# Two-stage Fourier transform and SoLU layer on one core: the order of scaled copies, first-transform products and block sums in a software pipeline

## Chip, core and metric

The kernel runs on one core of a Trainium2 chip. The time is that of the device for one execution, in microseconds (us); of several runs the median is taken. Before the change it is 1193.14 us (three runs, 1192.39 to 1193.9).

The core has five engines that take their instructions in order and wait for one another through semaphores: TensorE (PE, matmuls into PSUM; PEld is its weight load), VectorE (DVE), ScalarE (ACT), GpSimd (POOL) and SyncE (SP, which issues transfers here).

## What is computed

```python
def _attn_ref(x):                       # x: (8, 3136, 256), float32
    X = np.fft.fft(x, axis=1)
    X = np.fft.fft(X, axis=2)
    return X.real.astype(np.float32)

def _moe_ref(x, w_in, w_out, g_ln):     # x: (25088, 256), w_in: (256, 1024), w_out: (1024, 256)
    h = x @ w_in
    h_max = np.max(h, axis=-1, keepdims=True)
    e = np.exp(h - h_max)
    sm = e / (np.sum(e, axis=-1, keepdims=True) + 1e-09)
    solu = h * sm
    mu = np.mean(solu, axis=-1, keepdims=True)
    var = np.mean((solu - mu) ** 2, axis=-1, keepdims=True)
    ln = (solu - mu) / np.sqrt(var + 1e-06) * g_ln
    return (ln @ w_out).astype(np.float32)
```

The real part of the two-dimensional transform of each of eight sequences goes, as 25088 rows of 256, through a layer with 1024 hidden features: product, exponential against the row's maximum, a normalisation, product.

## The kernel before

The eight sequences are taken in four pairs. The transform along the sequence of 3136 = 49 x 64 is done in two parts. `transform1` (length 49) is done for a pair ahead of time, in 16 halves of 8 chunks: GpSimd adds the mirrored rows (`add_mirror`), VectorE folds the features (`fold`), TensorE multiplies, ScalarE copies the result `z` out, and it goes to DRAM and back. `transform2` (length 64) gives a *unit*: 128 rows of the spectrum, and with them 128 mirrored ones (signs 0 and 1). A pair has 25 units (the first has one sign), 100 in all, and step `i` of the main loop handles unit `i`:

- `up`: product with the input weights, in an even and an odd part, into PSUM banks of their own; `even` and `join` (VectorE) put the parts together for each sign and find the row's maximum;
- `expo` (ScalarE), `product` (VectorE: u = h times exponential), `square` and `stats` (ScalarE: variance), then a `pow` on GpSimd that gives the row's scale `rs`;
- `turn_blocks` (VectorE) and `move_blocks` (16 or 24 transfers) transpose u.

Four steps later (`lag`) comes the product with the output weights. A unit of even number takes it plainly (`down`: 16 matmuls of 256 columns for each sign), sign 1 one step `late`. A unit of odd number takes both signs at once as a 2 x 2 block product with seven block products instead of eight (`Down`), over two steps; it needs four sums `S` of blocks of u, which GpSimd makes. PSUM has four banks for results; `result(i)` is bank `i % 4`, and `bank(0..2)` are 2, 3 and 1.

```python
def transform1(pr, s):
    ...
    ps = result(0 if pr.p else s).rearrange("p (l d) -> p l d", l=2)
    ...                                   # four matmuls
    nc.scalar.copy(pr.z[:, l : l + 2, :], ps[0:ZR])
    if l == CH - 2:
        keep(pr, c, ...)                  # z to DRAM

def transform2(pr, k1):
    ...
    ps = result(0)[:, 0 : KD * P]         # four matmuls; take2 (ScalarE) copies them to q
    ...

def sums(t):                              # GpSimd
    A11, A12, A21, A22 = blocks(t)
    t.S = spool.tile([P, 4, KF // 2, P], FP32, tag="S", name="S")
    for j, (a, b, op) in enumerate(((A21, A22, ALU.add), (t.S[:, 0], A11, ALU.subtract),
                                    (A11, A21, ALU.subtract), (A12, t.S[:, 1], ALU.subtract))):
        nc.gpsimd.tensor_tensor(out=t.S[:, j], in0=a, in1=b, op=op)

class Down:                               # self.C11, self.X, self.P53 = banks 2, 3, 1
    ...
    def keep(self, s, half, ps):
        nc.scalar.mul(out=self.place(s, half), in_=ps, mul=self.t.rs[:, s : s + 1])
    # p1: C11 afresh         seed: X <- C11 (ScalarE)     p2: adds to C11, keep11 takes it
    # p4: P53 afresh, keep4  p5: P53 afresh, keep5        p3: P53 afresh
    # p6: adds to X, keep6   p7: adds to X                finish: VectorE adds P53 and X to ot
```

The main loop, whose order within each engine is the order of the program (cut):

```python
for i in range(whole + 1, len(units) + lag + 3):
    cur = units[i] if i < len(units) else None
    old = units[i - lag] if i < len(units) + lag else None
    seven = old and by_seven(i - lag)
    plain, late, scaled = late, None, []
    if i > whole + 2:
        store(units[i - lag - 3])
    if seven:
        sums(old)
    if done:
        done.finish()
        done = None
    if cur:
        enter(i)
        even(cur, up(cur, 0))
        cur.odd = up(cur, 1)
        second_transform(i + 2)           # transform2, take2, spread
        join(cur, 0)
        if 1 in cur.signs:
            join(cur, 1)
        expo(cur, 0)
    if seven:
        new = Down(old, i == whole + 1)
        new.p1()
        new.seed()
    if half:
        half.p5()
        half.p6()
    if cur and 1 in cur.signs:
        expo(cur, 1)
    if half:
        half.keep5()
        half.keep6()
    if plain:
        ps_o = down(*plain)
        ...
    if seven:
        new.p4()
        new.p2()
    elif old:
        ...                               # down(old, 0); sign 1 is late
    if half:
        half.p3()
        half.p7()
        half, done = None, half
    if cur:
        for s in cur.signs:
            product(cur, s)
        square(cur, 0)
    if plain:
        scale(*plain, ps_o)
    if cur and 1 in cur.signs:
        square(cur, 1)
    if seven:
        new.keep4()
        new.keep11()
        half = new
    if cur:
        other_pairs(i, ahead_pe)          # transform1 of the next pair
    if cur:
        for s in cur.signs:
            turn_blocks(cur, s)
        ...                               # move_blocks
        stats(cur)                        # ends with the pow on GpSimd
    for t, s, ps_o in scaled:
        scale(t, s, ps_o)
    if cur:
        ...                               # turn: z back from DRAM
        other_pairs(i, ahead)             # add_mirror, fold, load of the next pair
```

Of the kernel before, what the change touches and what calls it, by code (L numbers as in the profile page):

```python
# [35 lines left out]
def kernel(  # L36
# [241 lines left out]
    def stats(t):  # L278

        n = slice(0, len(t.signs))  # L280
        es2, v = (small.tile([P, 2], FP32, tag=tag, name=tag) for tag in ("es2", "v"))
        nc.scalar.activation(out=es2[:, n], in_=t.esum[:, n], func=ACT.Square, bias=limits[:, 3:4], scale=1e-3)
        for s in t.signs:
            nc.scalar.activation(out=v[:, s : s + 1], in_=t.ssq[:, s : s + 1], func=ACT.Identity, bias=es2[:, s : s + 1],  # L284
                                 scale=float(FF) ** -3)
        t.rs = small.tile([P, 2], FP32, tag="rs", name="rs")
        nc.gpsimd.tensor_tensor(out=t.rs[:, n], in0=v[:, n], in1=neg_half[:, n], op=ALU.pow)  # L287
# [145 lines left out]
    def down(t, s):  # L433

        uT = t.batch.uT[:, t.w].rearrange("p c i (n s) -> p c (i n) s", s=2)
        ps = (result(0) if s else bank(0))[:, 0:D]
        for c in range(KF):
            nc.tensor.matmul(ps, uT[:, c, :, s], Wo[:, c, :], start=(c == 0), stop=(c == KF - 1))  # L438
        return ps
# [5 lines left out]
    def store(t):  # L445

        for s in t.signs:
            if s:
                i = NP * NC + t.p * (NK - 1) + t.k1 - 1
                dma = nc.gpsimd.indirect_dma_start(  # L450
                    out=out, out_offset=bass.IndirectOffsetOnAxis(ap=idx[:, i : i + 1], axis=0),
                    in_=t.ot[s], in_offset=None)
            else:
                dma = nc.sync.dma_start(out=out_k[t.p, t.k1], in_=t.ot[s])

            tc.declare_no_dep(dma.ins, group=f"out{1 - s}", reason="other rows of the output")
            tc.add_to_no_dep_group(f"out{s}", dma.ins)
# [153 lines left out]
    START = [[2 + 2 * c for c in range(NC)], [4, 6, 8, 10, 12, 13, 15, 16]]  # L611

    def ahead(pr, step):

        start = START[pr.p == 1]
        if step == 0:
            load(pr, 0)
            load(pr, 1)
        for c in range(NC):
            if step == start[c]:  # L620
                add_mirror(pr, c, nc.gpsimd)
            if step == start[c] + 1:
                fold(pr, c)
                if c + 2 < NC:
                    load(pr, c + 2)

    def ahead_pe(pr, step):

        for c in range(NC):
            for half in range(2):  # L630
                if step == START[pr.p == 1][c] + 2 + half:
                    transform1(pr, c * CH // 2 + half)

    def turn_parts(pr, step):

        if step in (-5, -3, 2, 6, 11):
            turn(pr, (-5, -3, 2, 6, 11).index(step))

    with tc.manual_schedule():
# [102 lines left out]
        def other_pairs(i, do):  # L742
            cur = units[i]
            if cur.p + 1 < NP:
                do(pairs[cur.p + 1], cur.k1)
# [3 lines left out]
        for i in range(whole + 1):  # L749
# [23 lines left out]
            if i < whole:  # L773

                begin(i + 1)
                if 1 in cur.signs:
                    square(cur, 1)
                stats(cur)
            else:
                for s in cur.signs:  # L780
                    square(cur, s)
                    turn_blocks(cur, s)
                stats(cur)
                scale(units[0], 0, ps_o)
# [10 lines left out]
        half, done, late = None, None, None  # L795
        for i in range(whole + 1, len(units) + lag + 3):
# [4 lines left out]
            if i > whole + 2:  # L801
                store(units[i - lag - 3])
            if seven:
                sums(old)
            if done:
                done.finish()
                done = None
            if cur:
                enter(i)
                even(cur, up(cur, 0))  # L810
                cur.odd = up(cur, 1)
                second_transform(i + 2)
                join(cur, 0)
                if 1 in cur.signs:
                    join(cur, 1)
                expo(cur, 0)
# [4 lines left out]
            if half:  # L821
                half.p5()
                half.p6()
            if cur and 1 in cur.signs:
                expo(cur, 1)
            if half:
                half.keep5()
                half.keep6()
            if plain:
# [4 lines left out]
            if seven:  # L834
                new.p4()
                new.p2()
            elif old:
                order = old.signs[::-1] if old is units[-1] else old.signs
                scaled.append((old, order[0], down(old, order[0])))
                if len(order) == 2:  # L840
                    if old is units[-1]:
                        scaled.append((old, order[1], down(old, order[1])))
                    else:
                        late = (old, order[1])
# [10 lines left out]
            if cur and 1 in cur.signs:  # L855
                square(cur, 1)
# [4 lines left out]
            if cur:  # L861
                other_pairs(i, ahead_pe)
            if cur:
# [91 lines left out]
```

## Time and profile before

| | |
|---|---|
| time, median of three | 1193.14 us |
| span of the profiled execution | 1190.8 us |
| TensorE busy | 1140.4 us |
| VectorE busy | 1005.6 us |
| ScalarE busy | 763.2 us |
| GpSimd busy | 636.2 us |
| mean DMA rate | 156 GB/s |

How to read the profile: L12 is line 12 of the kernel as it was run. L182 is `transform1`, L210 `transform2`, L238 `up`, L252 `join`, L261 `expo`, L268 `product`, L275 `square`, L284 the end of `stats`, L287 the `pow`, L300 `turn_blocks`, L326 `move_blocks`, L350 `sums`, L355 the seven block products, L386 their scaled copies, L396 `seed`, L390 `finish`, L438 the plain product, L443 its scaled copy, L185 the copy of `z`, L216 that of `q`. A group's row has its busy time and the mean duration of one instruction; "idle before" is the time in which the engine had nothing to run ahead of it, with the work whose end released it. Matmuls overlap in the array, and their ends are modelled.

### The profile page before, as it was taken

The numbers are of one execution on the slowest core, as the hardware profiler recorded it, in microseconds if no ns is written. First come the engines' busy times: TensorE is split into PE (matmuls) and PEld (weight loads), VectorE is DVE, ScalarE is ACT, GpSimd is POOL, SyncE is SP. The second block draws the span as 40 slices with busy tenths as digits, with TensorE's granted clock in tenths as the row PEclk, the third lists the DMA queues.
The fourth block names the chain that finished last, engine by engine and source line by source line (L and its number), as shares of the span: only waits on it lengthen the run. The fifth ranks groups of instructions, "written<-read, shape, count | busy, mean of one in ns | idle before, by whom it ended". The sixth has DMA issues, their size and how long they took to land.

```text
span 1190.8 us, 18553 instructions
## 1 busy us (share of the span) xinstructions
PE 1140.4 (96%) x5850; PEld 884.2 (74%) x5850; DVE 1005.6 (84%) x1376; ACT 763.2 (64%) x1841; POOL 636.2 (53%) x558
## 2 busy tenths in 40 slices
PE   2888999999999999999999899999999999999998
PEld 1556777778777778778777678777788777778777
DVE  7889889888879898898988989898888898888870
ACT  3577666666657667666656666676675676677651
POOL 3035487745655757645556666746544264543444
PEclk9999999999999999999999999999999999999999
DMA  9771989956689787656789898886575785745553
GB/s 231 198 187 31 163 176 192 204 135 148 145 158 188 176 174 199 169 135 146 140 158 179 167 186 169 169 169 146 133 162 124 146 145 125 158 110 137 130 119 103
DMA packets 458465, 185.55 MB, mean 156 GB/s; under 512 B 425750, under 2 KB 440350, under 8 KB 458368
## 3 DMA queue, kind: packets, MB, share of 16 engines
q1 hardware_dynamic: 444608, 146.22, 58.6%
q0 software_dynamic: 13760, 38.16, 13.4%
q8 instruction: 47, 0.77, 0.3%
q14 instruction: 50, 0.41, 0.1%
HBM read 44.78 MB, written 38.80 MB: 70 GB/s over the span
## 4 chain that ended last, share of the span: by engine, by line
PE 74%; DVE 6%; DMA 5%; ACT 5%; SPq 4%; issue 3%; POOL 3%; DVEq 0%; POOLq 0%; ACTq 0%
PE ps_m L438 24%; PE ps_h L238 23%; PE ps_m L355 21%; PE ps_m L182 4%; SPq L326 3%; PE ps_m L210 3%; ACT u L261 3%; DMA room<-in_x_dram 2%; DMA uT<-v 2%; DVE u L268 2%; POOL S L350 1%; DVE h L252 1%; DVE v L300 1%; DMA F<-in_f_tab_dram 1%; DVE ev L244 1%
## 5 line engine op out<-in xcount | busy, mean ns | idle before, releaser
L438 PE MATMUL ps_m<-Wo,uT 128*128 128x256 f32 x1632 | 372.1, 382 | 3.6 <-ACT uT L317 2.1
L238 PE MATMUL ps_h<-Wi,q 128*128 128x512 f32 x800 | 360.5, 593 | 1.5 <-DVE nmax L252 1.5
L438 PEld LDWEIGHTS ps_m<-Wo,uT 128*128 128x128 f32 x1632 | 314.1, 197 | 33.8 <-ACT uT L317 2.4
L268 DVE SCALAR_TENSOR_TENSOR u<-h,u 128x1024 f32<-128x1024 f32 x196 | 296.9, 1526 | 32.0 <-ACT u L261 24.6
L287 POOL TENSOR_TENSOR rs<-v,neg_half 128x2 f32<-128x2 f32 (+1 forms) x100 | 75.9, 759 | 448.9 <-ACT v L284 433.0
L238 PEld LDWEIGHTS ps_h<-Wi,q 128*128 128x128 f32 x800 | 147.6, 190 | 149.3 <-issue 136.7
L275 ACT ACTIVATE h<-u,usum 128x1024 f32<-128x1024 f32 x196 | 223.9, 1144 | 45.1 <-DVE u L268 44.3
L261 ACT ACTIVATE u<-h,neg 128x1024 f32<-128x1024 f32 x196 | 225.3, 1150 | 6.4
L300 DVE STREAM_TRANSPOSE v<-u 128x1024 f32<-128x1024 f32 x192 | 227.4, 1223 | 0.1
L216 ACT COPY q<-ps_m 128x256 f32<-128x256 f32 x100 | 37.2, 372 | 203.3 <-PE ps_m L210 181.3
L244 DVE SCALAR_TENSOR_TENSOR ev<-w_mid,r,ps_h 128x1024 f32<-128x1024 f32 x100 | 127.3, 1273 | 47.4 <-PE ps_h L238 41.2
L252 DVE CUSTOM_DVE_ANT_0 h<-ev,ps_h 128x1024 f32<-128x1024 f32 x100 | 122.2, 1222 | 41.9 <-PE ps_h L238 34.9
L350 POOL TENSOR_TENSOR S<-uT 128x512 f32<-128x512 f32 x94 | 147.2, 1566 | 1.2
L355 PE MATMUL ps_m<-Ws,S 128*128 128x128 f32 x1128 | 143.3, 277 | 2.0 <-ACT ot L386 2.0
L355 PEld LDWEIGHTS ps_m<-Ws,S 128*128 128x128 f32 x1128 | 135.3, 194 | 2.7 <-issue 2.6
L252 DVE CUSTOM_DVE_ANT_0 h<-h,ps_h 128x1024 f32<-128x1024 f32 x96 | 117.3, 1222 | 14.2 <-ACT neg L259 0.5
L450 POOL DMA_INDIRECT out_dram<-ot,idx x96 | 105.7, 1102 | 35.3 <-issue 17.1
L355 PE MATMUL ps_m<-Wo,uT 128*128 128x128 f32 x752 | 104.4, 282 | 1.4 <-ACT ps_m L396 1.3
L182 PE MATMUL ps_m<-y,F 98*100 98x258 f32 (+3 forms) x288 | 73.6, 390 | 29.1 <-DVE y L130 24.1
L355 PEld LDWEIGHTS ps_m<-Wo,uT 128*128 128x128 f32 x752 | 96.3, 196 | 2.5 <-ACT ps_m L396 1.7
L210 PEld LDWEIGHTS ps_m<-T,g 128*128 128x128 f32 x400 | 60.1, 191 | 50.8 <-issue 45.0
L259 ACT ACTIVATE neg<-nmax 128x1 f32<-128x1 f32 x196 | 38.8, 198 | 82.2 <-DVE nmax L252 69.8
(87 smaller groups left out, 1160.1 us busy)
## 6 DMA issues: line engine op xcount, KB each, us to landing
uT<-v SPq DMA_DIRECT2D x752, 128.0 KB
out_dram<-ot SPq DMA_DIRECT2D x100, 128.0 KB
g<-zd POOLq DMA_DIRECT2D x72, 160.0 KB
xa<-in_x_dram SPq DMA_DIRECT2D x28, 392.0 KB
zd<-z SPq DMA_DIRECT2D x24, 400.0 KB
raw_in<-in_moe_w_in_dram SPq DMA_DIRECT2D x4, 512.0 KB
raw_out<-in_moe_w_out_dram SPq DMA_DIRECT2D x2, 1024.0 KB
r<-q SPq DMA_DIRECT2D x100, 0.5 KB
```

The source lines that it names most:

```text
L182: nc.tensor.matmul(o[..., cs], F[:, 2 * t + h, :], i[..., cs], start=first, stop=True, skip_group_check=True)
L238: nc.tensor.matmul(ps[:, fs], t.q[:, c * P : (c + 1) * P], Wi[:, c, fs], start=True, stop=True)
L244: nc.vector.scalar_tensor_tensor(out=t.ev, in0=w_mid, scalar=t.r, in1=ps, op0=ALU.mult, op1=ALU.add)
L252: nc.vector.tensor_tensor_reduce(out=t.h[s], in0=t.h[0] if s else t.ev, in1=t.odd, scale=1.0 if s else -0.5, scalar=-3.0e38, op0=ALU.add, ...
L261: nc.scalar.activation(out=t.u[s], in_=t.h[s], func=ACT.Exp, bias=t.neg[:, s : s + 1], accum_out=t.esum[:, s : s + 1])
L268: nc.vector.scalar_tensor_tensor(out=t.u[s], in0=t.h[s], scalar=1.0, in1=t.u[s], op0=ALU.mult, op1=ALU.mult, accum_out=t.usum[:, s : s + 1])
L275: nc.scalar.activation(out=t.h[s], in_=t.u[s], func=ACT.Square, bias=t.usum[:, s : s + 1], scale=-float(FF), accum_out=t.ssq[:, s : s + 1])
L300: nc.vector.transpose(out=t.batch.v[:, t.w, :, o], in_=t.u[s])
L350: nc.gpsimd.tensor_tensor(out=t.S[:, j], in0=a, in1=b, op=op)
L355: nc.tensor.matmul(o, a[:, c], b[:, c], start=start and c == 0, stop=c == n - 1, skip_group_check=True)
L438: nc.tensor.matmul(ps, uT[:, c, :, s], Wo[:, c, :], start=(c == 0), stop=(c == KF - 1))
L450: dma = nc.gpsimd.indirect_dma_start(out=out, out_offset=bass.IndirectOffsetOnAxis(ap=idx[:, i : i + 1], axis=0), in_=t.ot[s], in_offset=None)
```

## The change

Four things change their place; no matmul is added or taken away.

1. The scaled copies of the seven block products, `keep5` and `keep6`, stand ahead of the first and of the second exponential on ScalarE, so that TensorE gets their banks back sooner; `seed` stands ahead of the first exponential, and `keep4` and `keep11` ahead of the second square.
2. The two halves of a chunk in `transform1` are multiplied in one step, every second step: the first after the exponentials, the second at the step's end. All three pairs that are prepared ahead begin at a step of odd number (`SUMS`), so the products fall into even steps, in which bank 0 holds no plain product.
3. On GpSimd the `pow` of a unit moves behind the block sums of the next step (`power`), so that the sums don't wait for the end of the statistics; the stores come after both.
4. The last unit's two products get banks of their own.

```diff
+        t.v = v
+
+    def power(t):
+        n = slice(0, len(t.signs))
         t.rs = small.tile([P, 2], FP32, tag="rs", name="rs")
-        nc.gpsimd.tensor_tensor(out=t.rs[:, n], in0=v[:, n], in1=neg_half[:, n], op=ALU.pow)
+        nc.gpsimd.tensor_tensor(out=t.rs[:, n], in0=t.v[:, n], in1=neg_half[:, n], op=ALU.pow)
 ...
-    START = [[2 + 2 * c for c in range(NC)], [4, 6, 8, 10, 12, 13, 15, 16]]
+    SUMS = [None] + [[f + 2 * c for c in range(NC)] for f in (3, 27, 51)]
 ...                                      # ahead: add_mirror at SUMS, fold and load one step later
-    def ahead_pe(pr, step):
+    def ahead_pe(pr, i, half):
         for c in range(NC):
-            for half in range(2):
-                if step == START[pr.p == 1][c] + 2 + half:
-                    transform1(pr, c * CH // 2 + half)
+            if i == SUMS[pr.p][c] + 3:
+                transform1(pr, c * CH // 2 + half)
 
     def turn_parts(pr, step):
-        if step in (-5, -3, 2, 6, 11):
-            turn(pr, (-5, -3, 2, 6, 11).index(step))
+        at = (-4 if pr.p == 1 else -5, -3, 2, 6, 11)
+        if step in at:
+            turn(pr, at.index(step))
 ...
-            if i > whole + 2:
-                store(units[i - lag - 3])
+            kept = units[i - lag - 3] if i > whole + 2 else None
             if seven:
                 sums(old)
+            if fresh:
+                power(fresh)
+            fresh = cur
+            if kept:
+                for s in kept.signs:
+                    store(kept, s)
 ...
-                join(cur, 0)
-                if 1 in cur.signs:
-                    join(cur, 1)
-                expo(cur, 0)
+                for s in cur.signs:
+                    join(cur, s)
             if seven:
                 new = Down(old, i == whole + 1)
                 new.p1()
                 new.seed()
             if half:
                 half.p5()
+                half.keep5()
                 half.p6()
-            if cur and 1 in cur.signs:
-                expo(cur, 1)
+            if cur:
+                expo(cur, 0)
             if half:
-                half.keep5()
                 half.keep6()
+            if cur:
+                if 1 in cur.signs:
+                    expo(cur, 1)
+                other_pairs(i, ahead_pe, 0)
 ...
+            elif old is units[-1]:
+                for s in (1, 0):
+                    scaled.append((old, s, down(old, s, bank(2 * s)[:, 0:D])))
             elif old:
 ...
             if plain:
                 scale(*plain, ps_o)
-            if cur and 1 in cur.signs:
-                square(cur, 1)
             if seven:
                 new.keep4()
                 new.keep11()
                 half = new
             if cur:
-                other_pairs(i, ahead_pe)
-            if cur:
+                if 1 in cur.signs:
+                    square(cur, 1)
+                other_pairs(i, ahead_pe, 1)
                 for s in cur.signs:
                     turn_blocks(cur, s)
```

## The prediction

> **What bounds the kernel now.** I read the page's first part, then the table of stretches, the list of waits, and the timeline around each wait of TensorE. The first part names the engine:
>
> ```profile
> PE 1140.4 (96%) x5850; PEld 884.2 (74%) x5850; DVE 1005.6 (84%) x1376; ACT 763.2 (64%) x1841; POOL 636.2 (53%) x558
> ```
>
> TensorE (PE) is busy in 96% of the span, and the change leaves every matmul as it is. So it can only gain what TensorE waits, and the question is how much that is and where. The table of stretches gives it (length, PE busy, then the others; PEclk is the granted clock):
>
> ```profile
> 100.00:130.00 30.00, 27.30 (x131) 20.22 (x130) 24.85 (x33) 17.38 (x45) 18.48 (x17) 0.94 0.59 93
> 130.00:352.00 222.00, 220.10 (x1167) 173.46 (x1166) 191.26 (x256) 147.84 (x364) 137.15 (x113) 1.00 0.77 165
> 352.00:630.00 278.00, 275.80 (x1430) 215.95 (x1430) 244.27 (x325) 184.00 (x450) 165.56 (x141) 1.00 0.79 166
> 630.00:800.00 170.00, 165.00 (x856) 127.06 (x855) 151.76 (x197) 111.31 (x276) 109.21 (x90) 1.00 0.85 173
> 800.00:940.00 140.00, 139.54 (x740) 109.62 (x740) 120.07 (x165) 91.42 (x228) 69.36 (x64) 1.00 0.67 144
> 940.00:1150.00 210.00, 209.82 (x1089) 164.25 (x1088) 185.22 (x249) 142.22 (x348) 95.54 (x87) 1.00 0.62 133
> 1150.00:1191.00 41.00, 34.76 (x200) 31.76 (x199) 6.29 (x10) 9.27 (x24) 18.53 (x21) 0.96 0.38 100
> ```
>
> Length less PE busy: 2.7 us idle in 100 to 130, 1.9 in 130 to 352, 2.2, 5.0, 0.5, 0.2, and 6.2 in the last 41 us. The first 100 us (68.1 busy) are the set-up, which the change hardly touches. What ends these waits is ScalarE (ACT), late with a copy out of a PSUM bank that TensorE wants again. Three kinds, from the timeline (start, length, engine, line; in brackets the idle time before and who ended it):
>
> ```profile
> 404.66 0.46 ACT L443 ACTIVATE ot<-ps_m,rs 128x256 f32<-128x256 f32 x1
> 405.16 1.11 PE L182 MATMUL ps_m<-y,F 98*100 98x258 f32 x4 [1.25 <-ACT ot L443]
> ...
> 683.12 0.60 ACT L386 ACTIVATE ot<-ps_m,rs 128x128 f32<-128x128 f32 x2
> 683.62 1.13 PE L355 MATMUL ps_m<-Wo,S 128*128 128x128 f32 x8 [1.05 <-ACT ot L386]
> ...
> 228.20 0.58 ACT L185 COPY z<-ps_m 100x512 f32<-100x512 f32 x1
> 228.83 1.11 PE L182 MATMUL ps_m<-y,F 98*100 98x258 f32 x4 [1.10 <-ACT z L185]
> ```
>
> First: `transform1` wants bank 0 while the scaled copy of the late plain product (L443) still stands in it. Second: `p3` wants the bank of `p5`, whose scaled copy (L386) stands in ScalarE's queue behind both exponentials, and these behind VectorE's joins. Third: the second `transform1` wants bank 0 before `z` of the first is copied out.
>
> **What the Trainium skill says.** "Perfetto Trace Analysis", section "Tensor Engine Instruction (MATMUL, LD_WEIGHTS)": ScalarE, VectorE and GpSimd are strict FIFO, and a matmul's end is a modelled time. Both show here: L386 runs only after the second exponential though its product ended over 2 us earlier, and four matmuls that start 0.21 us apart are listed as one piece of 1.03 us, so a listed end is some 0.17 us after the true slot (an estimate: 1.03 less 4 x 0.215). A gap of TensorE is then worth its listed idle plus 0.17 us. "PSUM — Partial Sum Buffer", section "PSUM bank collisions raise a hardware error": two engines must be kept off one bank, so a copy that is late is a wait of TensorE, as above. "GPSIMD Engine Reference", section "8. Key points": GpSimd shares SBUF interfaces with VectorE and disturbs its instructions with two SBUF inputs. The trace agrees: the product L268 takes 1.22 us alone and 1.88 to 2.31 us beside the block sums L350, while the joins, which read PSUM, keep 1.22 us beside them. "TensorE: Matmul & The Clock Gate", section "What's actually happening": after an idle window of some 3.4 us the clock is halved. This trace shows the same after less: behind a wait of 2.17 us at 120.1 us and one of 1.96 us at 1153.8 us, the next matmuls take twice as long for about 3.3 us (rows of 8 in 1.80 and 1.91 us instead of 1.06). The measured gap decides.
>
> **How much there is.** 100 to 130 us: two waits (2.17 and 0.54 listed), with 0.17 for each 3.0, and the half clock 0.74 + 0.85 = 1.6: 4.6 us. 130 to 1150 us: idle 1.9 + 2.2 + 5.0 + 0.5 + 0.2 = 9.8 us in some 25 gaps, with 25 x 0.17 = 4.2 added: 14 us. The end: 1.96 and 0.56 listed (the second is the last unit's products waiting for bank 0), 2.9 with the 0.17s, and half clock 1.09 + 0.67 = 1.8: 4.7 us. **In all 23.3 us**, 2.0% of 1193.14. Everything else is matmuls in a row.
>
> **The change part by part.**
>
> *Scaled copies between the exponentials.* In the even step from 498.1 to 509.9 us of the timeline `p5` and `p6` are 16 matmuls from 501.98 to 503.93, so `p5` ends near 503.0. The first join is ready at 503.06. `keep5` at 503.0 costs 0.30 and puts the first exponential 0.2 us later; `keep6` before the second costs another 0.3, so the second exponential is some 0.7 us later and VectorE's second product with it. VectorE has this room: its step is 1.27 + 2 x 1.30 + 2 x 1.31 + 2.37 = 8.9 us, 10.3 with a fold, and the even step will last about 12.6. In return `p3` finds its bank free at 503.3 instead of 506.2, with its turn at 507. This removes the L386 waits: 0.46 + 1.05 + 0.90 + 0.79 + two small ones, with the 0.17s 4.2 us, and the one at 120.1 with its half clock, 3.9 us. `seed`, also ahead of the exponential now, removes 0.54 + 0.76 listed, 1.6 us with the 0.17s. `keep4` and `keep11` ahead of the second square remove the 1.96 at 1153.8: in that step they ran from 1153.34 behind a square that ended at 1153.25, and would run at 1151.6, just when `p5` wants the bank.
>
> *Products of the first transform two at a time.* Eight matmuls at 0.215 = 1.72 us per two steps, before as after: no work saved. In even steps bank 0 holds no plain product, so the L443 waits (0.08 + 1.25 + 0.48 + small ones, 3.4 us with the 0.17s) go. The two products are set apart by a plain product and `p3`, `p7`: 3.4 + 1.8 = 5.2 us in which `z` (0.58) is copied right behind the second exponential, near 507 of 510. This removes the L185 waits: 1.10 + 0.68 + 1.01 listed, 3.3 us. The even step grows from 11.8 to about 12.6 us, and the odd one (509.9 to 521.1) shrinks from 11.2 to about 10.4; their sum stays.
>
> *Block sums first, `pow` behind them.* GpSimd waits 433 us in all for ScalarE's `v` at the head of its queue:
>
> ```profile
> POOL rs L287 <- ACT v L284: 433.0, 90, 14.1
> ```
>
> In the odd steps this wait goes, and the four sums (6.1 us, contended) start when `p7` gives S back, instead of about 3.5 us into the step. They then lie beside `ev` and the joins, which are not slowed, instead of the two products, which lose 0.7 to 1.1 us each. VectorE's busy time should fall by about 20 to 40 us of its 1005.6. None of it is on TensorE's path by itself; it is slack for the squares and copies that follow. In the 24 steps with a fold the sums meet the fold instead (0.64 + 0.67 alone, 0.83 + 1.76 beside sums at 652 us), so a part is given back there.
>
> *The start times of the pairs* all become odd. Now they are even for the second and the fourth pair of sequences and odd for the third; the stretch of the fourth (630 to 800 us) has 5.0 us of idle, that of the third (352 to 630) 2.2. So the change gives all the better phase.
>
> *The end.* The last unit's two products use banks 2 and 1 instead of 0: the 0.56 at 1180 goes.
>
> *The sum.* 130 to 1150: of 14 us about 1.9 stay, namely the waits for the copy of `q` (two of 0.46) and one 0.11 around units with one sign; about 1.5 I keep for new waits. Gain 10.5. 100 to 130: gain 3.5 of 4.6. End: gain 3.5 of 4.7, because unit 98's blocks move only after 1151.9 (16 transfers, the last issued at 1163.2), and a TensorE that is 4 us earlier reaches them with about 0.5 us to spare. Together 17.5; less 1.5 for what I can't see: 16. **1193.1 - 16 = 1177 us.**
>
> **The rivals.** *A: the waits only change places.* With every copy ahead of an exponential, ScalarE's queue waits for TensorE, and VectorE for ScalarE. VectorE's pair of steps is 17.8 + 1.4 fold + 0.9 sums of products + up to 2 contention, 22.1 us beside TensorE's 23.0. If contention stays at its size and the exponentials come 0.7 us later each, VectorE becomes the bound in the fold steps; 24 of them at 0.5 us are 12 us, and the time is 1186 to 1192. For it: VectorE at 89% in 630 to 800 us. Against it: where the phase is already odd, at 352 to 630, the waits are small, and joins can lag TensorE by some 5 us before `up` is held. *B: moving the sums takes the contention to the even step.* If S comes free part by part already after `p6`, the sums start 5 us earlier, beside the even step's products, and nothing is gained on VectorE; the order on ScalarE alone then makes the time about 1181. *C: the waits vanish altogether*, with the end and 120 us: 1193.1 - 23.3 = 1170. *D: the second transform is late*, since the tables of the second pair are read one step later, two steps before their use: one wait of up to 5 us. The transfers have over 20 us, so I give it little.
>
> **Range and chances.** C is the floor, since nothing below the back-to-back matmuls can be had: 1170. A gives the upper end, 1187. A gain of over 2% (below 1169.3) needs more than all the waits: 4%. A loss of over 2% would need half a microsecond of new wait in each of 48 pairs of steps beyond today's: 2%. The rest, 94%, is within 2%, and within it I hold faster for far likelier than not.
>
> **What would show it.** PE busy stays at 1140 within a few us, and idle of TensorE in 130 to 1150 falls from 9.8 to under 3 us. L386, L443 and L185 vanish from what ends waits of TensorE. The wait of L287 for L284 falls by about half. L268's mean falls from 1526 ns to 1300 to 1430. The granted clock in 100 to 130 us is 0.98 or more. It is wrong if waits of TensorE for VectorE (nmax, L252) or for `ot` L390 turn up in every fold step, or if L268's mean stays.

## The result, and the profile after

The changed kernel takes **1178.33 us** (median of 6, 1176.4 to 1180.07), beside 1191.9 us (median of 6, the three that the prediction began with among them) of the kernel before. The ratio is 0.9888, with a 95% interval of 0.987 to 0.9906: 1.1% less time. The prediction had 1177.

In the new program's line numbers `stats` still ends at L284; the `pow` is L291, `uT` is moved at L330, the sums are L354, the seven products L359, their scaled copies L390, `finish` L394, `seed` L400, the plain product L443, its scaled copy L448, the indirect store L454 and the plain store L458. Lines up to L282 keep their numbers.

The first part of the page, busy time of each engine:

```profile
PE 1132.6 (96%) x5850; PEld 881.2 (75%) x5850; DVE 1005.7 (86%) x1376; ACT 762.4 (65%) x1841; POOL 598.2 (51%) x558
```

TensorE's sum is 7.8 us lower with the same 5850 matmuls, so no work was saved. Cut at the same units, 1.3 us of it lie in the set-up and 2.0 from unit 99 on, where matmuls at half clock stood before. Of the 4.5 us between, the half clock after 120 us is 1.6 by the prediction's estimate; the rest I read as the listed ends, some 0.17 us late for each piece, since 11 waits cut the row of matmuls there instead of 22. VectorE (DVE) did not get lighter by a tenth of a microsecond.

The table of stretches, columns as before (length, PE busy, the other engines, PEclk third from the end):

```profile
100.00:130.00 30.00, 28.36 (x155) 22.27 (x154) 28.02 (x38) 18.96 (x48) 24.27 (x21) 1.00 0.77 147
130.00:352.00 222.00, 221.66 (x1173) 174.74 (x1172) 199.10 (x261) 148.61 (x366) 126.43 (x115) 1.00 0.80 168
352.00:630.00 278.00, 277.08 (x1447) 217.58 (x1446) 247.62 (x326) 186.10 (x458) 154.76 (x142) 1.00 0.81 166
630.00:800.00 170.00, 167.89 (x881) 131.16 (x880) 159.98 (x203) 110.29 (x278) 107.54 (x89) 1.00 0.87 173
800.00:940.00 140.00, 139.54 (x716) 108.23 (x715) 115.84 (x162) 94.39 (x229) 60.27 (x62) 1.00 0.64 141
940.00:1150.00 210.00, 209.85 (x1134) 168.00 (x1133) 170.37 (x241) 139.37 (x343) 91.26 (x93) 1.00 0.58 132
```

Idle of TensorE from 130 to 1150 us is 0.34 + 0.92 + 2.11 + 0.46 + 0.15 = 4.0 us; it was 9.8. At 100 to 130 us the clock is 1.00 instead of 0.94: the wait of over 2 us and the half clock after it are gone. What ended TensorE's waits in the kernel before, from its list of waits (total us, times, longest):

```profile
PE ps_m L355 <- ACT ot L386: 7.3, 6, 2.2
PE ps_m L182 <- ACT z L185: 1.8, 2, 1.1
PE ps_m L182 <- ACT ot L443: 1.7, 2, 1.3
...
PE ps_m L210 <- ACT z L185: 1.0, 1, 1.0
```

What still ends them, and under it GpSimd's (POOL) wait for `v`:

```profile
PE ps_m L182 <- ACT q L216: 2.2, 5, 0.8
PE ps_h L238 <- DVE nmax L252: 2.1, 3, 0.8
PE ps_m L359 <- ACT ot L390: 1.8, 2, 1.0
...
POOL rs L291 <- ACT v L284: 251.7, 51, 14.1
```

Two of the three old kinds, the scaled copy L443 of before and `z` L185, are gone from the main loop. The third is not: L390 here is the scaled copy L386 of before, and two of its waits are left, 0.80 us at 108.9 and 0.98 us at 665.7. `transform1` now waits instead for the copy of `q`, which comes out of bank 0 too (2.2 us in five waits). Of the waits for `nmax` only one of 0.57 us lies after the set-up. GpSimd's wait for `v` fell from 433.0 to 251.7 us.

At the end something new stands. The timeline of the last stretch (start, length, engine, line), first of the kernel before:

```profile
1180.10 7.18 PE L438 MATMUL ps_m<-Wo,uT 128*128 128x256 f32 x32 [0.56 <-ACT ot L443]
...
1184.75 0.96 POOL L450 DMA_INDIRECT out_dram<-ot,idx  x1 [2.32 <-ACT ot L443]
```

And of the changed one:

```profile
1157.24 10.53 PE L443 MATMUL ps_m<-Wo,uT 128*128 128x256 f32 x48
1161.01 0.98 POOL L454 DMA_INDIRECT out_dram<-ot,idx  x1 [2.50 <-DMA out_dram<-ot,idx]
1164.16 0.96 POOL L454 DMA_INDIRECT out_dram<-ot,idx  x1 [2.18 <-issue]
1167.32 0.96 POOL L454 DMA_INDIRECT out_dram<-ot,idx  x1 [2.19 <-issue]
1170.50 0.96 POOL L454 DMA_INDIRECT out_dram<-ot,idx  x1 [2.22 <-issue]
```

The last matmul ends at 1167.8. GpSimd's stores follow each other every 3.2 us, the last begins at 1170.5, and the span ends at 1174.4: 6.7 us after TensorE, where it was 3.5 us. TensorE has got ahead of the row of stores.

**Where the time came from.** The traces are cut at the first `up` matmul of a unit, so that equal work is compared. "Preparing" is the sum of the three stretches in which a later pair of sequences is prepared (units 5 to 21, 28 to 46, 53 to 75); "end" is from unit 99 to the end of the span. "After, again" is a second profile of the changed kernel; the other rows are experiments described below. All in us.

| kernel | set-up, to unit 5 | 5-21 | 28-46 | 53-75 | preparing | end | span |
|---|---|---|---|---|---|---|---|
| before | 100.7 | 188.0 | 204.3 | 250.3 | 642.6 | 48.8 | 1190.8 |
| after | 97.1 | 182.7 | 202.8 | 246.2 | 631.8 | 47.4 | 1174.4 |
| after, again | 100.8 | 181.2 | 202.8 | 246.2 | 630.2 | 48.3 | 1177.5 |
| order alone | 99.0 | 185.0 | 206.6 | 247.3 | 639.0 | 49.9 | 1186.0 |
| pairs alone | 98.9 | 183.9 | 202.4 | 244.1 | 630.4 | 48.9 | 1176.9 |
| sums alone | 98.5 | 193.2 | 230.8 | 245.2 | 669.2 | 47.2 | 1212.9 |
| odd starts alone | 100.0 | 184.9 | 205.3 | 246.7 | 636.9 | 49.0 | 1185.1 |
| pairs, even starts | 98.2 | 183.2 | 203.7 | 248.6 | 635.4 | 48.9 | 1181.5 |
| without the sums' part | 99.6 | 181.8 | 202.4 | 243.5 | 627.7 | 47.8 | 1173.2 |
| whole, even starts | 99.0 | 182.5 | 202.5 | 244.9 | 629.8 | 46.4 | 1173.4 |
| stores in the gap | 97.0 | 181.9 | 202.4 | 243.8 | 628.1 | 46.1 | 1169.3 |

The change brought 10.8 and 12.4 us in the preparing stretches in its two profiles, and 1.4 and 0.5 us at the end. The set-up, which no version alters in its work, lies anywhere between 97 and 101 us, also for one and the same program; 3 us of a single profile's difference can be that.

### The profile page after: what moved, and what is told of

It is laid out like the page before. It is cut to its first block, busy times and chain, and to the rows that moved or that the text cites. A ratio compares the mean times of both kernels' runs of the same rounds, so it can differ in the third digit from the quotient of the medians.

```text
span 1174.4 us, 18577 instructions
## 1 busy us (share of the span) xinstructions
PE 1132.6 (96%) x5850; PEld 881.2 (75%) x5850; DVE 1005.7 (86%) x1376; ACT 762.4 (65%) x1841; POOL 598.2 (51%) x558
## 3 DMA queue, kind: packets, MB, share of 16 engines
q0 software_dynamic: 13760, 38.16, 12.4%
## 5 line engine op out<-in xcount | busy, mean ns | idle before, releaser
L443 PE MATMUL ps_m<-Wo,uT 128*128 128x256 f32 x1632 | 369.2, 380 | 3.1 <-ACT uT L321 2.1
L443 PEld LDWEIGHTS ps_m<-Wo,uT 128*128 128x128 f32 x1632 | 314.2, 196 | 33.8 <-ACT uT L321 2.4
L268 DVE SCALAR_TENSOR_TENSOR u<-h,u 128x1024 f32<-128x1024 f32 x196 | 266.1, 1366 | 50.5 <-ACT u L261 36.1
L354 POOL TENSOR_TENSOR S<-uT 128x512 f32<-128x512 f32 x94 | 130.4, 1387 | 208.5 <-issue 138.7
L261 ACT ACTIVATE u<-h,neg 128x1024 f32<-128x1024 f32 x196 | 225.3, 1150 | 6.4
L291 POOL TENSOR_TENSOR rs<-v,neg_half 128x2 f32<-128x2 f32 (+1 forms) x100 | 71.7, 717 | 251.8 <-ACT v L284 251.7
L359 PE MATMUL ps_m<-Ws,S 128*128 128x128 f32 x1128 | 141.5, 275 | 1.8 <-ACT ot L390 1.8
L359 PEld LDWEIGHTS ps_m<-Ws,S 128*128 128x128 f32 x1128 | 133.6, 192 | 2.7 <-issue 1.6
L454 POOL DMA_INDIRECT out_dram<-ot,idx x96 | 100.8, 1050 | 30.7 <-issue 18.7
L359 PE MATMUL ps_m<-Wo,uT 128*128 128x128 f32 x752 | 104.2, 282 | 0.1
L210 PEld LDWEIGHTS ps_m<-T,g 128*128 128x128 f32 x400 | 60.2, 191 | 49.1 <-issue 41.7
L359 PEld LDWEIGHTS ps_m<-Wo,uT 128*128 128x128 f32 x752 | 96.1, 196 | 0.9 <-issue 0.5
```

The lines of the kernel that those rows point to most:

```text
L261: nc.scalar.activation(out=t.u[s], in_=t.h[s], func=ACT.Exp, bias=t.neg[:, s : s + 1], accum_out=t.esum[:, s : s + 1])
L268: nc.vector.scalar_tensor_tensor(out=t.u[s], in0=t.h[s], scalar=1.0, in1=t.u[s], op0=ALU.mult, op1=ALU.mult, accum_out=t.usum[:, s : s + 1])
L359: nc.tensor.matmul(o, a[:, c], b[:, c], start=start and c == 0, stop=c == n - 1, skip_group_check=True)
L454: dma = nc.gpsimd.indirect_dma_start(out=out, out_offset=bass.IndirectOffsetOnAxis(ap=idx[:, i : i + 1], axis=0), in_=t.ot[s], in_offset=None)
```

## The experiments

The first question was which part brings the gain. The theory: waits of TensorE for ScalarE vanish, the order and the pairs each taking their own kinds. The rivals: waits only change places, or it is the starts on odd steps.

**1. The order on ScalarE alone**, on the kernel before (this diff and those that follow are shortened).

```diff
-                expo(cur, 0)              # and expo(cur, 1), ahead of the copies
             if half:
                 half.p5()
+                half.keep5()
                 half.p6()
+            if cur: expo(cur, 0)
+            if half: half.keep6()
+            if cur and 1 in cur.signs: expo(cur, 1)
-            square(cur, 1)                # moves behind keep4, keep11
```

> The kernel before with ScalarE's new order alone: seed and keep5 ahead of the first exponential, keep6 ahead of the second, keep4 and keep11 ahead of the second square. Theory W (the gain is TensorE's waits for copies, each part takes its own kind): the waits ended by the scaled copies L386 and by seed go, those ended by L443 and by the copy of z stay: 4.2 us in the main loop, 0.9 for seed, about 3.5 at 107 to 120 us, 3 to 4 at 1153 us with the half clock; 9 to 11 us, ratio 0.991 to 0.993. Rival V (ScalarE is late because VectorE is, and VectorE because GpSimd's block sums slow its products): the order only moves the waits, at most 3 us, ratio 0.997 or more.

Measured: 1187.85 us, ratio 0.9976 (0.9967 to 0.9986), 3.0 us, as the rival had it. Preparing gains 3.6 us, but the stretch 28 to 46 loses 2.3 and the end 1.1. Of its waits of TensorE:

```profile
PE ps_m L182 <- ACT ot L443: 5.4, 9, 1.4
PE ps_m L355 <- POOL S L350: 2.5, 2, 2.3
```

L386 falls from 7.3 us in this list to one wait of 1.0, but L443, the scaled plain copy, rises from 1.7 to 5.4. One of them in this run's timeline:

```profile
466.42 3.30 DVE L268 SCALAR_TENSOR_TENSOR u<-h,u 128x1024 f32<-128x1024 f32 x1 [0.36 <-ACT u L261]
469.76 1.15 ACT L275 ACTIVATE h<-u,usum 128x1024 f32<-128x1024 f32 x1 [2.01 <-DVE u L268]
470.91 0.45 ACT L443 ACTIVATE ot<-ps_m,rs 128x256 f32<-128x256 f32 x1
471.41 1.11 PE L182 MATMUL ps_m<-y,F 98*100 98x258 f32 x4 [1.37 <-ACT ot L443]
```

VectorE's product takes 3.30 us beside GpSimd's sums (1.23 us alone), the square waits for it, the copy waits behind the square in ScalarE's queue, and `transform1` waits for the copy's bank. So a part of the gain does change places. At the end, TensorE comes to the block products of unit 97 before GpSimd has summed them (`S` L350, 2.31 us), and the wait that the order was to remove there returns under another name.

**2. The products two at a time alone**, with the odd starts that belong to them.

```diff
+    SUMS = [None] + [[f + 2 * c for c in range(NC)] for f in (3, 27, 51)]
+            if i == SUMS[pr.p][c] + 3:
+                transform1(pr, c * CH // 2 + half)
+            if cur: other_pairs(i, ahead_pe, 0)     # behind the second exponential
-                other_pairs(i, ahead_pe)
+                other_pairs(i, ahead_pe, 1)
```

> The kernel before with the first transform's products two at a time and the odd starts alone; ScalarE's order and GpSimd's order as before, but for the copies of z, which follow their products. Theory W: the waits for L443 and for z go (6.7 us), a few of the L386 kind grow because ScalarE's queue is fuller in even steps: 3 to 6 us, ratio 0.995 to 0.9975. Rival V: VectorE has the same work and the same contention, so under 2 us.

Measured: 1177.55 us, ratio 0.9891 (0.9872 to 0.9909). This part alone brings what the whole change brings. In the main loop no wait for L443 or L386 is left (one of L386, 1.95 us, and one of L443, 0.56 us, stand in the end); two waits behind `seed` (L396) stay, 3.1 us, one of them 2.34 us at 107 us with half clock behind it:

```profile
PE ps_m L355 <- ACT ps_m L396: 3.1, 2, 2.3
...
PE ps_m L355 <- ACT ot L386: 1.9, 1, 1.9
```

**3. The order on GpSimd alone.**

```diff
+            if seven:
+                sums(old)
+            if fresh:
+                power(fresh)
+            fresh = cur
             if i > whole + 2:
                 store(units[i - lag - 3])
-            if seven:
-                sums(old)
```

> The kernel before with GpSimd's order alone: block sums ahead of the power and the stores, the power of a unit one step later. Theory W: VectorE's product L268 falls from a mean of 1526 ns to about 1350, but TensorE doesn't wait for VectorE, so 0 to 3 us, ratio 0.9975 to 1.000. Rival V: this is the source, 6 to 10 us, ratio 0.992 to 0.995.

Measured: 1213.44 us, ratio 1.0182 (1.016 to 1.0205): slower by 22.6 us, which neither theory expected. The stretch 28 to 46, where the starts are odd, loses 26.5 us, and 53 to 75, where they are even, gains 5.1; 5 to 21, where they are even but for two, loses 5.2. Two lines of its table of stretches, 350 to 625 (which holds all of the first) and 625 to 790:

```profile
350.00:625.00 275.00, 257.61 (x1276) 197.41 (x1275) 231.14 (x295) 166.94 (x413) 139.05 (x125) 0.96 0.70 151
625.00:790.00 165.00, 163.31 (x860) 127.75 (x859) 140.47 (x195) 108.42 (x269) 101.38 (x93) 1.00 0.81 176
```

TensorE idles 17.4 us in the first and its clock falls to 0.96. An odd step from there (L447 is the scaled plain copy in this program):

```profile
486.90 2.36 POOL L137 TENSOR_TENSOR xa<-xa,xb 98x1020 f32<-98x1020 f32 x1
487.67 2.69 DVE L268 SCALAR_TENSOR_TENSOR u<-h,u 128x1024 f32<-128x1024 f32 x1 [0.17 <-ACT u L261]
490.40 1.15 ACT L275 ACTIVATE h<-u,usum 128x1024 f32<-128x1024 f32 x1 [1.20 <-DVE u L268]
491.55 0.45 ACT L447 ACTIVATE ot<-ps_m,rs 128x256 f32<-128x256 f32 x1
492.05 1.11 PE L182 MATMUL ps_m<-y,F 98*100 98x258 f32 x4 [2.10 <-ACT ot L447]
```

It is the chain of experiment 1 with another cause. With its block sums done early, and with the `pow` of the same step no longer ahead of them, GpSimd comes to the **mirrored sums of the next pair** (L137) right in the odd step, beside the first product. In the kernel before they ran in the even step that follows, at 500.79 us, behind the `pow` at 500.08. Product, square, scaled copy and `transform1` are late one after the other; and since several of the waits are now over 2 us long (2.88 us at 411.5, four of 2.09 to 2.10 us at 438.4 to 518.9), the clock halves behind some of them. The prediction looked at what the block sums would no longer disturb, and not at what GpSimd would do in the time it gained. In the whole change no wait of this kind is listed: `transform1` no longer wants bank 0 in odd steps.

The second question: is the sums' part of any use within the whole change, and what did it cost?

**4. The whole change without the sums' part**: `pow` and the stores stand ahead of the sums, as before, though the `pow` of a unit stays in the next step.

```diff
-            if seven:
-                sums(old)
             if fresh:
                 power(fresh)
             fresh = cur
             if kept: ...                  # the stores
+            if seven:
+                sums(old)
```

> The changed kernel with GpSimd's power and stores put back ahead of the block sums (the power still in the next step). Theory W: within 2 us of the changed kernel, ratio to before 0.988 to 0.991; the mean of L268 back over 1480 ns. Rival V: most of the gain is lost, ratio 0.995 or more.

Measured: 1174.2 us, ratio 0.9861 (0.984 to 0.9882). The changed kernel's median is 1178.33, its ratio 0.9888; the intervals overlap, but the extremes of the two kernels' times (1173.02 to 1175.19 and 1176.4 to 1180.07) don't. Preparing lasts 627.7 us, 2.5 to 4.1 less than with the sums' part. So this part costs some 3 to 4 us; the two kernels were timed on different chips, each beside the kernel before. The mean of VectorE's product L268 is back at 1551 ns, so its fall was the work of this part. On the same chip experiment 2 took 1177.55 us: beside the pairs the order on ScalarE, with the small rest of the change, still brings some 3 us, and the sums' part takes as much away. That is why the pairs alone come out level with the whole change.

**5. The changed kernel again**, on the chip of the next three.

> The changed kernel as it is, for a comparison on the same chip as the next three: ratio 0.987 to 0.990. If moving the block sums first really costs about 4 us within the change (theory T, from the kernel without it at 1174.2 us), it stays over 1176 us.

Measured: 1177.45 us, ratio 0.989 (0.9867 to 0.9913). Its profile repeats the preparing stretches within 1.6 us, its set-up is 3.7 us longer.

**6. The whole change with even starts**: mirrored sums in even steps, fold in odd ones, products in even steps as before.

```diff
-    SUMS = [None] + [[f + 2 * c for c in range(NC)] for f in (3, 27, 51)]
+    SUMS = [None] + [[f + 2 * c for c in range(NC)] for f in (4, 28, 52)]
-            if i == SUMS[pr.p][c] + 3:
+            if i == SUMS[pr.p][c] + 2:
```

> The changed kernel with the mirrored sums one step later, in even steps, and the folds between, in odd steps; the products of the first transform stay in the same steps. The block sums then meet no fold, and the mirrored sums meet the joins instead of the first product. Theory T (the new order on GpSimd costs time because its sums fall on the folds and its mirrored sums on the first product of the odd step): the mean of L268 falls to 1230 to 1290 ns, the folds to 0.65 us, VectorE's busy time from 1005 to under 955 us, the waits for scaled copies behind p4 and for nmax go, ratio 0.984 to 0.987. If contention on VectorE is not the cause, the ratio stays at 0.988 to 0.990.

Measured: 1174.17 us, ratio 0.9862 (0.9838 to 0.9885), 3.3 us under the changed kernel on the same chip. VectorE's groups (busy us, mean ns) of the changed kernel, product and the two instructions of the fold:

```profile
L268 DVE SCALAR_TENSOR_TENSOR u<-h,u 128x1024 f32<-128x1024 f32 x196 | 266.1, 1366 | 50.5 <-ACT u L261 36.1
...
L128 DVE TENSOR_TENSOR y<-xa 98x508 f32<-98x508 f32 x28 | 26.6, 950 | 0.1
...
L129 DVE TENSOR_TENSOR y<-xa 98x508 f32<-98x508 f32 x28 | 40.4, 1443 | 0.0
```

And of this one:

```profile
L268 DVE SCALAR_TENSOR_TENSOR u<-h,u 128x1024 f32<-128x1024 f32 x196 | 255.3, 1306 | 54.6 <-ACT u L261 37.2 <-issue 11.2
...
L128 DVE TENSOR_TENSOR y<-xa 98x508 f32<-98x508 f32 x28 | 18.3, 653 | 0.1
...
L129 DVE TENSOR_TENSOR y<-xa 98x508 f32<-98x508 f32 x28 | 19.0, 680 | 0.0
```

With odd starts the fold lies at the end of the even step, exactly where the block sums now begin, and takes about twice as long; with even starts it takes what it takes alone. VectorE's busy time falls from 1005.7 to 961.0 us, the saving that the prediction had expected of the change itself (1306 ns and 961.0 us are a little above what was expected here). That 45 us of VectorE go with no more than 3.3 us of time shows how far off the path they were.

**7. Odd starts alone**, products one at a time.

```diff
-    START = [[2 + 2 * c for c in range(NC)], [4, 6, 8, 10, 12, 13, 15, 16]]
+    START = [None] + [[f + 2 * c for c in range(NC)] for f in (3, 2, 3)]
```

> The kernel before with the odd starts alone: one product of the first transform in each step as before. Theory T (what pays is that no product of the first transform stands at the end of an odd step, behind the scaled copy of the plain product in bank 0): the waits for L386 around 640 to 780 us go, those for L443 come in their place, 0 to 4 us in all, ratio 0.9965 to 1.000. Rival U (the odd phase of GpSimd's and VectorE's extra work is what pays, since the third pair had it before and waited least): most of the gain of the two-at-a-time kernel, ratio 0.989 to 0.992.

Measured: 1186.42 us, ratio 0.9958 (0.9946 to 0.997), between the two theories; preparing gains 5.7 us.

```profile
PE ps_m L355 <- ACT ot L386: 3.9, 3, 2.0
PE ps_m L182 <- ACT ot L443: 3.1, 3, 2.3
```

**8. Two at a time with even starts**: experiment 2 with `SUMS` of (4, 28, 52) and `+ 2`.

```diff
-    SUMS = [None] + [[f + 2 * c for c in range(NC)] for f in (3, 27, 51)]
+    SUMS = [None] + [[f + 2 * c for c in range(NC)] for f in (4, 28, 52)]
-            if i == SUMS[pr.p][c] + 3:
+            if i == SUMS[pr.p][c] + 2:
```

> The kernel before with the products two at a time in the same even steps, but the mirrored sums in even steps and the folds in odd ones; the orders of ScalarE and GpSimd as before. Theory T: the gain stays, ratio 0.988 to 0.992. Rival U: most of it is lost, ratio 0.995 or more.

Measured: 1184.25 us, ratio 0.9955 (0.9935 to 0.9975); preparing gains 7.2 us. With 7 that makes 12.9 us, and experiment 2, which does both, has 12.2: **the two at a time and the odd starts are two gains that add**, each about half. (By the medians they make 4.2 + 6.4 = 10.6 us beside 13.3; the intervals allow for the difference.) What each leaves is plain from the lists of waits. In units 5 to 99, odd starts alone leave 3.1 us of L443 and 1.9 of L386; two at a time with even starts leave no L443, but 5.7 us of L386 (and 1.95 in the end):

```profile
PE ps_m L355 <- ACT ot L386: 7.6, 9, 2.0
```

The last question was the end of the program.

**9. The last six units' stores one step sooner**, in the changed kernel, behind `finish`.

```diff
-    for i in range(whole + 1, len(units) + lag + 3):
+    for i in range(whole + 1, len(units) + lag + 2):
...
             if done:
                 done.finish()
+            if not cur:
+                ...                       # the stores of units[i - lag - 2]
```

> The changed kernel with the last six units' stores issued one step sooner, behind the sums of products that make them ready; nothing else. If GpSimd's row of stores, 3.2 us each, is what ends the changed kernel (its last matmul ends 6.7 us before the span's end, against 3.5 us before the change), the time from the last matmul to the end falls to 3.5 to 4.5 us and the whole by 2.5 to 3.5 us, ratio 0.985 to 0.987. If the stores only follow the last product, under 1 us.

Measured: 1178.05 us, ratio 0.9885 (0.9862 to 0.9908): nothing. The first store of the row still stands behind the last block sums in GpSimd's queue (1154.12 us), the second waits 4.09 us for `finish` (until 1159.22), and four more follow at no less than 3.15 us each. So the row ends as late as it did, and from the last matmul to the end it is 7.3 us.

**10. The same with sums behind `pow` and stores in the main loop** (experiment 4 with the last six units' stores sooner).

```diff
-            if kept: ...                  # the stores, ahead of the sums
+            if cur: ...                   # the same, in the main loop only
             if seven:
                 sums(old)
             if done:
                 done.finish()
+            if not cur: ...               # the stores of units[i - lag - 2]
```

> The kernel with the change's order on ScalarE and its products two at a time, but the power and the stores ahead of the block sums as before, plus the sooner stores at the end, where the block sums then come first. From the kernel without the sums' part (1174.2 us): the wait of 2.3 us for S near 1151 us with what follows it goes, about 3 us: 1171 us, ratio 0.982 to 0.985.

Measured: 1174.56 us, ratio 0.9864 (0.9843 to 0.9886). TensorE reaches its end earlier, unit 99 to last matmul 41.3 us instead of 44.0 in experiment 4, and what follows it grows from 3.8 to 6.6 us: the gain is given back.

**11. Experiment 6 with the same stores sooner** (the edit of experiment 9 on it).

```diff
-            if kept: ...
+            if cur: ...
             if done:
                 done.finish()
+            if not cur: ...
```

> The changed kernel with the mirrored sums in even steps and the sooner stores at the end: from 1174.2 us of the kernel with even mirrored sums, 1 to 2 us less, since its end after the last matmul is 5.5 us: 1172 to 1173 us, ratio 0.983 to 0.986. If VectorE's busy time mattered to the total this one, with 45 us less of it, would beat the one with the sums in their old place; I expect the two within 2 us.

Measured: 1173.81 us, ratio 0.9861 (0.9839 to 0.9884), as experiment 6.

**12. Two stores moved out of the row**: in experiment 10 those of units 93 and 94 go ahead of the last unit's block moves, where GpSimd waits for TensorE anyway.

```diff
+                if i == len(units) - 1:
+                    for u in units[i - lag - 2 : i - lag]:
+                        for s in u.signs:
+                            store(u, s)
                 if i >= len(units) - 2:
                     move_blocks ...
```

> The kernel with the power ahead of the block sums and the end's stores one step sooner, in which the stores of units 93 and 94 now come in the last unit's own step, where GpSimd waits for TensorE before it moves that unit's blocks; so the row of six stores behind the last block sums has one less and starts at once. If that row (3.2 us for each store) ends the kernel, the time from the last matmul to the end falls from 6.6 us to 3.5 to 4.5 us, and the whole to 1171 to 1172.5 us, ratio 0.982 to 0.9845. If it does not, 1174 us as before.

Measured: 1172.72 us (1171.2 to 1174.78), ratio 0.9862 (0.9838 to 0.9885). From its timeline:

```profile
1154.61 10.53 PE L443 MATMUL ps_m<-Wo,uT 128*128 128x256 f32 x48
...
1165.11 0.96 POOL L454 DMA_INDIRECT out_dram<-ot,idx  x1 [2.20 <-issue]
```

The last store now starts as TensorE's last matmul ends, where in the changed kernel it starts 2.7 us later, and the stretch after the last matmul falls from experiment 10's 6.6 to 4.1 us. This shows the row of stores as the bound there. The ratio itself doesn't set this version apart from experiments 4, 6 and 11; all four are faster than before, and their medians lie below the changed kernel's.

## Why the prediction was right, and where it was not

**The total and the idea held.** TensorE was the bound and the gain was its waits: L443 and `z` went, L386 fell from 7.3 to 1.8 us. The pool of 14 us in 130 to 1150 plus 4.6 in 100 to 130 was taken as a gain of 10.5 + 3.5, less 1.5 for the unseen, so 12.5 us; the preparing stretches gave 10.8 and 12.4. That this held while its shares did not (9.7 us for the order, which brought 3.0 to 3.6 alone, and 6.7 for the pairs, which brought 12.2) is partly luck.

**Order on ScalarE: its share was oversized.** The L386 waits (4.2 us), the one at 120 us (3.9) and `seed` (1.6) were put down to it, 9.7 us. Alone it brings 3.6 us of preparing and 3.0 us of time. The step that failed is the one-to-one assignment of a wait to the part that moves the copy named in it. Rival A is half right for this part alone: L443 rises from 1.7 to 5.4 us. Beside the pairs the order has less to do, as odd starts had removed most L386 waits already (5.4 to 1.9 us in units 5 to 99).

**Pairs: undersized.** 6.7 us were given to them, and the "better phase" of the starts got no number. Together they bring 12.2 us of preparing, some 7 and 6 us each. The remark on the odd starts was the right observation (5.0 us idle in the stretch of the fourth pair, 2.2 in that of the third), but it should have been a term of the sum. Why a start in even steps makes L386 late can be read in the trace of before. All five of its L386 waits in units 5 to 99 (at 120.1, 660.7, 683.6, 707.6 and 777.8 us) stand in even steps that begin with a fold on VectorE:

```profile
676.50 0.64 DVE L128 TENSOR_TENSOR y<-xa 98x508 f32<-98x508 f32 x1
...
677.07 0.67 DVE L129 TENSOR_TENSOR y<-xa 98x508 f32<-98x508 f32 x1
...
677.67 1.26 DVE L244 SCALAR_TENSOR_TENSOR ev<-w_mid,r,ps_h 128x1024 f32<-128x1024 f32 x1
```

The fold is ahead of `ev`, `ev` of the joins, the joins of both exponentials, and behind these stands the copy, here at 683.12 us. In the stretch of the fourth pair `ev` began 3.7 us (mean) after the step's first `up` matmul in the 8 even steps with a fold, and 2.0 us after it in the 3 without. With odd starts the fold goes to the odd steps. Experiments 8 and 2 differ in that and in the mirrored sums, which move along; between them the 5.7 us of L386 vanish.

**Sums first: the mean came, the saving didn't.** L268 fell to 1366 ns, inside 1300 to 1430, and gave 30.8 us. VectorE's groups in the kernel before, beside those shown in experiment 6:

```profile
L268 DVE SCALAR_TENSOR_TENSOR u<-h,u 128x1024 f32<-128x1024 f32 x196 | 296.9, 1526 | 32.0 <-ACT u L261 24.6 <-issue 1.0
...
L129 DVE TENSOR_TENSOR y<-xa 98x508 f32<-98x508 f32 x28 | 21.1, 753 | 0.0
L128 DVE TENSOR_TENSOR y<-xa 98x508 f32<-98x508 f32 x28 | 19.7, 702 | 0.1
```

The term that was mis-sized is the fold, "a part is given back there": L128 and L129 rose from 40.8 to 67.0 us on `xa`, and other work took the rest, so VectorE's busy time stayed at 1005.7. The prediction had both numbers of the fold (0.64 + 0.67 alone, 0.83 + 1.76 beside the sums) and 24 folds, and did not multiply them: 24 x 1.28 = 31 us, the whole of what the products gain. In one fold step the crowding is followed by waits of TensorE:

```profile
654.46 1.55 DVE L128 TENSOR_TENSOR y<-xa 98x508 f32<-98x508 f32 x1
655.93 1.52 DVE L129 TENSOR_TENSOR y<-xa 98x508 f32<-98x508 f32 x1
...
662.34 1.96 PE L238 MATMUL ps_h<-Wi,q 128*128 128x512 f32 x4 [0.57 <-DVE nmax L252]
...
665.72 2.02 PE L359 MATMUL ps_m<-Ws,S 128*128 128x128 f32 x16 [0.98 <-ACT ot L390]
```

The first wait, for VectorE's `nmax`, is what the prediction named as rival A's sign. The second is not: its `ot` L390 is VectorE's `finish` in the numbers of before, while this L390 is a scaled copy on ScalarE (L386 of before), behind a square that waited for VectorE's product. A wait for `nmax` stands in this one fold step of the main loop and in no other, so A stayed small. Experiment 4 puts the cost of the part at 3 to 4 us on the whole; that it is this contention which costs them is supported by experiment 6, not isolated.

**Rival B** (the sums start behind `p6`) fell: in that step of the changed kernel they start at 652.57 us, released by a product L359, and `p7` had started at 651.43. **Rival D** (second transform late) fell too: the list has for its products L210 only 0.9 us for `q` and one of 0.3 for a transfer, both in the set-up.

**The end: 3.5 us predicted, 1.4 and 0.5 found.** TensorE's part did shorten, from 45.3 to 40.7 us, more than thought. The step that failed is that the span follows TensorE there: GpSimd's stores set it. So of the 16 us predicted the medians show 13.6, and the 2.4 us that are missing are about what the end fell short by. The time is still only 1.3 us from the number, by luck: all six runs of before have a median 1.2 us under the three that the sum began with. (Between the two first profiles lie 16.4 us, 3.6 of them set-up, as in the table.)

**The signs named.** TensorE busy was to stay at 1140 "within a few us": 1132.6, for the reasons given above. Idle under 3 us: 4.0. L386 was to vanish with L443 and L185: 1.8 us of it stay. L287's wait by half: to 58%. Clock at least 0.98: 1.00. Rival C's floor of 1170, a ratio of 0.981, was not passed; the least ratio here is 0.9861 (experiments 4 and 11).

## What to carry to other kernels

When TensorE is nearly always busy, list its waits and what ends each; but don't credit each wait to the edit that moves the instruction named in it, since one wait may have two cures and a cured wait may uncover the next. An engine off the path that is given free time does its next work earlier: before reordering its queue, ask beside what that next work will then lie. And at a program's end look at the row of transfers separately: they may have a pace of their own that a faster engine doesn't change.

## What the runs showed of the hardware

- Indirect stores of 128 KB on GpSimd's queue follow each other every 3.15 to 3.2 us: 0.96 us for the instruction, then 2.2 us in which nothing visible is waited for. The Trainium skill, "DMA: Bandwidth & Descriptors", section "Anatomy of one DMA — SWDGE (gpsimd) path", gives a fit of 2.0 us plus bytes over 436 GB/s for one transfer from this queue, an estimate of 2.3 us here. It is of the size of the gap; that the gap is this completion was not shown. In the changed kernel the store of 1161.01 us landed 2.4 us after its start, 0.75 us before the next one began, so the landing alone does not fill the gap.
- The Trainium skill, "GPSIMD Engine Reference", section "8. Key points", names a contention of GpSimd with VectorE for SBUF, without a size. Here VectorE's product took 1.23 us alone and up to 3.30 us beside GpSimd's sums (in the kernel before, 1.86 us on average and at most 2.52 where the block sums lay beside nearly all of it). A block sum took 1.03 to 1.54 us with neither product nor fold beside it, and up to 2.51 us beside the product.
- A half clock followed waits of 2.17 us (before, 120.1) and 1.96 us (before, 1153.8): within 1 us the matmuls of 128 columns came 0.21 us apart. It did not follow waits of the same lengths elsewhere, 2.17 us (sums alone, 118.4) and 1.96 us (odd starts alone, 1148.0), nor one of 2.32 us (without the sums' part, 1151.3): there they came 0.11 us apart. So the length of the wait alone doesn't decide it.
